# Four edits to a fused state-space and gated-layer gradient kernel: the order of k's loads, the width of ssm_k's transposes, the engine of one copy, the order of the last gradient

## The chip, the cores and the metric

The kernel runs on one core of a Trainium2 chip. A core has five engines that run side by side, each with its own queue, taken in order: TensorE (PE; matrix products and transposes, with weight loads listed apart as PEld), VectorE (DVE), ScalarE (ACT), GpSimd (POOL) and SyncE (SP), which here issues nearly all DMA transfers. TensorE writes into PSUM, a small accumulation memory, and ScalarE or VectorE copy results from there to SBUF, the working memory. The metric is the time of one execution on the device in microseconds (us); the lower the better.

## The reference

With sequence length S = 2048, width D = 512 and F = 1376, the forward function is

```python
xn = layernorm(A_q)
k_shift[s] = sum_t k[s - t'] * shift_k[:, t']        # four taps
kv = k_shift * v
y  = causal_conv(kv, ssm_k) + kv * ssm_D             # by FFT of length 2S in the reference
A  = xn * y
B  = ((xn @ w_gate) * (xn @ w_up)) @ w_down
out = x + A + B
```

The reference returns `out` and, for a given `grad_out`, the gradients of q, k, v, shift_k, ssm_k, ssm_D, w_gate, w_up and w_down: ten outputs, all bf16. In the kernel's numbering out_2 and out_3 are the gradients of k and v, out_4 to out_6 those of shift_k, ssm_k and ssm_D, out_7 to out_9 those of w_gate or w_up (two) and w_down.

## The kernel before

The sequence is laid out as `nat`: position s = 16 p + r sits in partition p (128 of them) at row r of R = 16. The long convolution is a two-stage Fourier transform by matrix products. In a first stretch (`front`, `pre`, `kernel_spec`) three signals (ssm_k, kv and the product of grad_out and xn) pass through `stage1` (TensorE into `pf`, copied to `fst`, stored to DRAM as `FD`). In a second (`groups`) they are loaded again as `X`, transformed, multiplied on VectorE and transformed back into `GD`, again in DRAM. Beside all this runs the gated layer over eight chunks of 256 positions (`ffn1`, `yb`). In the last stretch (`dw` with its side generators) TensorE computes the weight gradients over 11 blocks of F (10 of 128, the last of 96) and the second half of the inverse transforms.

The code lists work in the order of generators, which hand over at each `yield`. A scheduler then places the instructions of each engine; `tc.high_priority` moves some ahead, and `tc.issue_after(i)` keeps what is inside behind instruction i in that placing. On the chip each engine and each DMA queue runs its list strictly in that order.

These are the places that the change touches:

- `kernel_spec` (L405) reads `ssk`, ssm_k as loaded: 512 channels in 4 groups of 128 partitions, 2048 positions along the free axis. Helper `tr` turns four rows r at a time: 16 transposes of 128x128, each reading every 16th element (32 bytes apart), into one PSUM tile `ptk`. ScalarE copies it to `kn` (L235 is the line of the helper `act`, L238 that of `dve`), which the first stage reads. The two buffers of `kn` are shared with `skt`, the broadcast taps of the shift.
- `hds` are the two buffers of the gated layer's products; `hd1` is used by odd chunks.
- `inv_y` (L919) alternates the inverse transform of y and of the gradient towards kv for four rows at a time, from tiles `g` loaded out of `GD` by `load_g1` (L775). `load_vk` loads v and the shifted k (`KS`). VectorE forms the gradient towards shifted k (`dks`) and v (`kb`, stored as out_3, L939).
- `load_kh` (L1104) loads k once more as `khC`, with three rows of the neighbour partition: one load of 2 MB (L1108) and two of 336 and 45 KB. `dsk_gram` (L1027) multiplies `dks` with it on TensorE (`pk`, L1033) for the gradient of shift_k.
- `ew` runs `final` and `bwd` for each pair of rows: VectorE's work for out_0, out_1 and out_2, fed by `load_fin` (`bb`, L1072).
- `inv_dk` (L955) makes the gradient of ssm_k: `gk` loaded from `GD`, products `po`, copied by ScalarE to `o5t`. Its position 0 is the gradient of ssm_D: `put_dD` (L975) copies it to `dDs`, transposes it (`ptd`) and stores it.
- `dw` (L984) takes for each block of F first the gradient of w_down (`pd`, 16 matmuls of 512 columns, copied to `od`, stored), then those of w_up and w_gate (`pu`, 64 matmuls, copied to `og`, stored).

Of the kernel before, what the change touches and what calls it, by code (L numbers as in the profile page):

```python
# [8 lines left out]
BF = mybir.dt.bfloat16  # L9
F32 = mybir.dt.float32  # L10
I32 = mybir.dt.int32
ALU = mybir.AluOpType
# [178 lines left out]
def kernel(  # L191
# [39 lines left out]
    def cs(c):  # L231
        return slice(c * 128, (c + 1) * 128)

    def act(o, i):
        nc.scalar.copy(o, i)  # L235
# [16 lines left out]
    def P2(name, shape, dt=F32):  # L252
        return ps2.tile(shape, dt, name=name, tag="p2")

    def P1(name, shape, dt=F32):
        return ps1.tile(shape, dt, name=name, tag="p1")
# [27 lines left out]

    hds = [p.tile([P, NFB, 3, 256], BF, name=f"hd{i}") for i, p in enumerate((hdp, hdl))]

    tab_es = ExitStack()
    TB = Tables(nc, const, wY, tab_es.enter_context(tc.tile_pool(name="tabt", bufs=1, side="right")))
    for t in hds:
# [114 lines left out]

    def kernel_spec():  # L405
        def tr(r0):
            pt = P2("ptk", [P, 4, D], BF)
            for i in range(4):
                for c in range(NC4):
                    src = ssk[:, c, :].rearrange("d (p r) -> d r p", r=R)[:, r0 + i, :]  # L410
                    nc.tensor.transpose(pt[:, i, cs(c)], src, ident[:])
            kn = ST["st1"].tile([P, 4, D], BF, name="kn", tag="kn", bufs=KNB)
            with tc.high_priority(offset=SOON):
                act(kn[:], pt[:])
            return kn
        kn = tr(0)
        yield
        for r0 in range(0, R, 4):
            for i in range(4):
                stage1(0, kn, i, r0 + i, act if i % 2 else dve)  # L420
                if i == 1 and r0 + 4 < R:
                    nx = tr(r0 + 4)
                yield
            kn = nx
# [204 lines left out]
    def seq(*its):  # L629
        for it in its:  # L630
            for _ in it:
                yield
# [176 lines left out]
    def nat_h(fb, r):  # L809
        f0, fw = FBLK[fb]  # L810
        if fb not in TURNED:
            return nats[fb, 0][:, r, :fw]
        return nats[fb, 0][:, r // 2, 0, r % 2, :] if r < R - 2 else nats[fb, 1][:, 0, r % 2, :fw]
# [96 lines left out]
    def load_vk(r0):  # L910
        vb = c2b.tile([P, 2, D], BF, name="vb")
        nc.sync.dma_start(vb[:], v_n[:, r0:r0 + 2, :])
        kb = c2b.tile([P, 2, D], BF, name="kb")
        nc.sync.dma_start(kb[:], KS[:, r0:r0 + 2, :])
        return vb, kb

    DKS = {}
# [1 line left out]
    def inv_y():  # L919
        gq = pend  # L920
        todo = [(sg, r0) for r0 in range(0, R, 4) for sg in (0, 1)][2:]
        for r4 in range(0, R, 4):
            gy = gq.pop(0)
            vk = [load_vk(r4), load_vk(r4 + 2)]
            for i in range(0, 4, 2):
                st1p(gy, i, yC[:, r4 + i:r4 + i + 2, :])
            if todo:
                gq.append(load_g1(*todo.pop(0)))
            yield
            gd = gq.pop(0)  # L930
            for i in range(0, 4, 2):
                r0 = r4 + i
                vb, kb = vk.pop(0)
                dd = c2b.tile([P, 2, D], BF, name="dd")
                st1p(gd, i, dd[:])
                with tc.high_priority(offset=SOON):
                    DKS[r0] = nc.vector.tensor_tensor(dks[:, r0:r0 + 2, :], dd[:], vb[:], op=ALU.mult)
                    nc.vector.tensor_tensor(kb[:], dd[:], kb[:], op=ALU.mult)
                nc.sync.dma_start(o3_n[:, r0:r0 + 2, :], kb[:])  # L939
                if r0 == 2:  # L940
                    nc.gpsimd.memset(dks[96:128, R:R + 3, :], 0.0)
                    nc.sync.dma_start(dks[0:112, R:R + 3, :], dks[1:113, 0:3, :])
                    nc.sync.dma_start(dks[112:127, R:R + 3, :], dks[113:128, 0:3, :])
            if todo:
                gq.append(load_g1(*todo.pop(0)))
            yield
# [8 lines left out]
    def inv_dk():  # L955
        o5t = c2.tile([P, NC4, P, R], BF, name="o5t", tag="o5k")
        o5 = out_5.rearrange("(c q) s -> c q s", q=P)
        steps = [(dh, rh) for dh in range(2) for rh in range(2)]
        for n, (dh, rh) in enumerate(steps):
            gk = gks.pop(0)  # L960
            for b in range(2):
                po = P2("po", [P, 8, P])
                for i in range(8):
                    for c in range(2):
                        nc.tensor.matmul(po[:, i, :], lhsT=gk[:, c, i, cs(b)], rhs=TB.IW[:, c, :], start=(c == 0), stop=(c == 1))
                act(o5t[:, 2 * dh + b, :, 8 * rh:8 * rh + 8], po[:].rearrange("q r s -> q s r"))
                if rh == 1:
                    nc.sync.dma_start(o5[2 * dh + b], o5t[:, 2 * dh + b].rearrange("q s r -> q (s r)"))
                if b == 1 and n + 2 < len(steps):
                    gks.append(load_gk(*steps[n + 2]))  # L970
                yield
            if n == 2:
                yield from put_dD(o5t)

    def put_dD(o5t):  # L975
        nc.vector.tensor_copy(dDs[:], o5t[:, :, 0, 0])
        yield
        pt = P1("ptd", [P, P], BF)
        nc.tensor.transpose(pt[:NC4, :], dDs[:], ident[:])
        dDt = c2.tile([NC4, P], BF, name="dDt")  # L980
        dve(dDt[:], pt[:NC4, :])
        nc.sync.dma_start(out_6.rearrange("(c p) -> c p", p=128), dDt[:])

    def dw():  # L984
        og = None
        load_hb(2)
        for fb, (f0, fw) in enumerate(FBLK):
            last = fb + 1 == NFB
            pd = P1("pd", [P, D])
            for r in range(R):  # L990
                nc.tensor.matmul(pd[:fw, :], lhsT=nat_h(fb, r), rhs=goC[:, r, :], start=(r == 0), stop=(r == R - 1))  # L991
            od = c2b.tile([P, D], BF, name="od")
            act(od[:fw], pd[:fw])
            nc.sync.dma_start(out_9[f0:f0 + fw, :], od[:fw])
            yield
            if not last:
                hid_t(fb + 1, 0)
                yield
                hid_t(fb + 1, 1)
                yield  # L1000
            pu = P2("pu", [P, NC4, 2, P])
            if fb % 2 == 0:
                og = c2.tile([P, 2, NC4, 2 * P], BF, name="og")
            q0 = (fb % 2) * P
            for c in range(NC4):
                for r in range(R):
                    nc.tensor.matmul(pu[:, c, :, :fw], lhsT=xnC[:, r, cs(c)], rhs=nat_d(fb, r),  # L1007
                                     start=(r == 0), stop=(r == R - 1))
                if c == 1:
                    yield  # L1010
                    if not last:
                        hid_t(fb + 1, 2)
                        if fb + 3 in TURNED:
                            load_t(fb + 3)
                        elif fb + 3 < NFB:
                            load_hb(fb + 3)
                        yield
            act(og[:, :, :, q0:q0 + fw].rearrange("p t c f -> p c t f"), pu[:, :, :, :fw])
            if fb + 1 in TURNED:
                last_t(fb + 1)  # L1020
            if fb % 2 == 1 or last:
                a = f0 - q0
                for t, o in enumerate((out_7, out_8)):
                    nc.sync.dma_start(o[:, a:f0 + fw].rearrange("(c p) f -> p c f", p=128), og[:, t, :, :q0 + fw])
            yield

    def dsk_gram():  # L1027
        for c in range(NC4):
# [75 lines left out]
    def load_kh():  # L1104
        khC = c2.tile([P, R + 3, D], BF, name="khC", tag="o5k")
        nc.gpsimd.memset(khC[0:1, 0:3, :], 0.0)
        with tc.issue_after(DKS[10].ins):
            nc.sync.dma_start(khC[:, 3:3 + R, :], k_n)  # L1108
            nc.sync.dma_start(khC[1:113, 0:3, :], k_n[0:112, R - 3:R, :])
            nc.sync.dma_start(khC[113:128, 0:3, :], k_n[112:127, R - 3:R, :])  # L1110
        KH.append(khC)
        yield

    def every(gen, start, step):
        return [start, step, gen]
# [16 lines left out]
    def load_dk():  # L1132
        gks.append(load_gk(0, 0))
        gks.append(load_gk(0, 1))
        yield

    sides = [every(seq(inv_y(), load_kh(), load_dk()), 0, 3), every(dsk_gram(), 27, 2), every(inv_dk(), 35, 3), every(ew(), 7, 3)]
    for n, _ in enumerate(dw()):
        for sd in sides:
            if n >= sd[0]:  # L1140
# [35 lines left out]
```

## Time and profile before

| | |
|---|---|
| median of 3 runs | 497.99 us (497.42 to 498.01) |
| profiled execution | 496.1 us, span 494.2 us |
| TensorE busy | 472.5 us, 96% of the span |
| weight loads / VectorE / ScalarE / GpSimd busy | 314.4 / 339.8 / 317.4 / 13.8 us |
| DMA | 140.39 MB moved, mean 284 GB/s |
| granted TensorE clock | 0.995 of full speed |

All comes from one profiled execution. A row of the timeline gives start, length, engine, line, what is written and from what, and in brackets how long the engine was idle before and what ended that. Matmuls are pipelined: the length of one is the time until its result is there, while the next starts long before. So how often matmuls start is read from groups, not from single lengths. "SPq" rows are the issue of a DMA on SP's queue; when the data arrives is told apart, as time to landing.

### The profile page before, as it was taken

The numbers are of one execution on the slowest core, as the hardware profiler recorded it, in microseconds if no ns is written. First come the engines' busy times: TensorE is split into PE (matmuls) and PEld (weight loads), VectorE is DVE, ScalarE is ACT, GpSimd is POOL, SyncE is SP. The second block draws the span as 40 slices with busy tenths as digits, with TensorE's granted clock in tenths as the row PEclk, the third lists the DMA queues.
The fourth block names the chain that finished last, engine by engine and source line by source line (L and its number), as shares of the span: only waits on it lengthen the run. The fifth ranks groups of instructions, "written<-read, shape, count | busy, mean of one in ns | idle before, by whom it ended". The sixth has DMA issues, their size and how long they took to land.

```text
span 494.2 us, 10487 instructions
## 1 busy us (share of the span) xinstructions
PE 472.5 (96%) x4331; PEld 314.4 (64%) x4331; DVE 339.8 (69%) x623; ACT 317.4 (64%) x352; POOL 13.8 (3%) x29
## 2 busy tenths in 40 slices
PE   7789999999999999999999999999998989999986
PEld 7676764547647548447447744567676668877775
DVE  6679979987383768667786873018239999996740
ACT  4668896849748678779779963566575535453221
POOL 4400000000000000000000000020000000000000
PEclk9899999999999999999999999999999999999999
DMA  9998999899997966978968298999998899999823
GB/s 272 376 403 297 291 271 336 309 326 329 342 266 244 275 192 205 292 252 256 306 207 270 74 342 308 388 324 385 366 352 290 336 309 347 272 248 245 251 97 110
DMA packets 112523, 140.39 MB, mean 284 GB/s; under 512 B 33306, under 2 KB 86879, under 8 KB 110940
## 3 DMA queue, kind: packets, MB, share of 16 engines
q1 hardware_dynamic: 111004, 138.41, 86.6%
q10 hardware_dynamic: 1472, 1.31, 0.8%
q8 instruction: 34, 0.56, 0.5%
q14 instruction: 13, 0.11, 0.1%
HBM read 68.97 MB, written 63.41 MB: 268 GB/s over the span
## 4 chain that ended last, share of the span: by engine, by line
PE 60%; DMA 15%; DVE 13%; ACT 4%; SPq 3%; issue 2%; POOL 1%; ACTq 0%; DVEq 0%
PE pgu L513 12%; PE px L556 12%; PE pu L1007 8%; PE pdh L519 5%; DMA g<-GD 5%; PE py L549 5%; PE pd L991 4%; PE pt L834 3%; PE pg L614 3%; DMA x_b<-in_A_q_dram 2%; PE ps L585 2%; PE pf L366 2%; DMA out_dram<-dk 2%; PE pq L907 2%; PE pk L1033 2%
## 5 line engine op out<-in xcount | busy, mean ns | idle before, releaser
L556 PE MATMUL px<-WT,hd 128*128 128x512 bf16 (+1 forms) x352 | 81.0, 380 | 0.0
L1007 PEld LDWEIGHTS <-xnC 128*128 128x128 bf16 x704 | 67.3, 98 | 8.3 <-issue 0.3
L556 PEld LDWEIGHTS <-hd 128*128 128x128 bf16 (+1 forms) x352 | 32.8, 98 | 44.1 <-issue 7.4
L1007 PE MATMUL pu<-natd,xnC 128*128 128x256 bf16 x512 | 58.8, 273 | 0.2 <-ACT nath L235 0.2
L513 PE MATMUL pgu<-xt,Wu 128*128 128x256 bf16 (+1 forms) x352 | 54.0, 277 | 3.6 <-ACT gu L235 3.3
L235 ACT CAST GO<-pg 128x1024 bf16<-128x1024 f32 x48 | 46.2, 1015 | 17.5 <-PE pg L614 12.9
L235 ACT CAST SP<-ps 128x1024 bf16<-128x1024 f32 x48 | 46.5, 1028 | 11.9 <-PE ps L585 7.8
L235 ACT CAST gu<-pgu 128x1024 bf16<-128x1024 f32 (+1 forms) x48 | 45.4, 945 | 13.4 <-PE pgu L513 11.9
L513 PE MATMUL pgu<-xt,Wg 128*128 128x256 bf16 (+1 forms) x352 | 53.5, 275 | 0.0
L601 DVE TENSOR_TENSOR T<-SP 128x2048 bf16<-128x2048 bf16 x24 | 29.4, 1223 | 28.7 <-ACT SP L235 26.1
L519 PE MATMUL pdh<-gt,WdT 128*128 128x256 bf16 (+1 forms) x352 | 47.6, 273 | 0.1
L513 PEld LDWEIGHTS <-Wu 128*128 128x128 bf16 (+1 forms) x352 | 33.3, 101 | 19.1 <-issue 14.2
L235 ACT CAST fst<-pf 128x1024 bf16<-128x1024 f32 x40 | 39.1, 1035 | 3.8 <-issue 2.6
L549 PE MATMUL py<-Wd,hd 128*128 128x512 bf16 (+1 forms) x176 | 41.3, 379 | 0.0
L235 ACT COPY natd<-pt 128x2048 bf16<-128x2048 bf16 x16 | 30.0, 1873 | 14.8 <-PE pt L834 14.8
L519 PEld LDWEIGHTS <-WdT 128*128 128x128 bf16 (+1 forms) x352 | 34.9, 100 | 5.4
L513 PEld LDWEIGHTS <-Wg 128*128 128x128 bf16 (+1 forms) x352 | 35.3, 101 | 4.1
L235 ACT CAST og<-pu 128x1024 bf16<-128x1024 f32 (+1 forms) x11 | 10.9, 993 | 39.4 <-PE pu L1007 25.5
L533 DVE TENSOR_TENSOR hd<-gu 128x512 bf16<-128x512 bf16 (+1 forms) x48 | 19.1, 398 | 23.4 <-ACT gu L235 23.3
L534 DVE TENSOR_TENSOR hd<-gu,dh 128x1024 bf16<-128x1024 bf16 (+1 forms) x48 | 30.9, 643 | 1.4 <-ACT dh L235 0.4
L549 PEld LDWEIGHTS <-hd 128*128 128x128 bf16 (+1 forms) x176 | 16.6, 98 | 20.4 <-issue 2.5
L601 DVE TENSOR_TENSOR U<-SP 128x2048 bf16<-128x2048 bf16 x24 | 29.2, 1218 | 0.0
(166 smaller groups left out, 693.2 us busy)
## 6 DMA issues: line engine op xcount, KB each, us to landing
HDD<-hd SPq DMA_DIRECT2D x35, 384.0 KB, 3.8
FD<-fst SPq DMA_DIRECT2D x24, 512.0 KB, 4.5
X<-FD SPq DMA_DIRECT2D x24, 512.0 KB, 5.1
GD<-GO SPq DMA_DIRECT2D x24, 512.0 KB, 3.3
hb<-HDD SPq DMA_DIRECT2D x8, 1344.0 KB, 10.0
g<-GD SPq DMA_DIRECT2D x8, 1024.0 KB, 7.2
bb<-BX SPq DMA_DIRECT2D x8, 512.0 KB, 6.4
gk<-GD SPq DMA_DIRECT2D x4, 1024.0 KB, 8.5
```

The costliest lines, as they stand in the source:

```text
L235: nc.scalar.copy(o, i)
L513: nc.tensor.matmul(pgu[:w, i, t, :], lhsT=W[:, c, f0:f0 + w], rhs=xt[:, :, c, :], start=(c == 0), stop=(c == NC4 - 1))
L519: nc.tensor.matmul(pdh[:w, i, :], lhsT=WdT[:, c, f0:f0 + w], rhs=gt[:, :, c, :], start=(c == 0), stop=(c == NC4 - 1))
L533: nc.vector.tensor_tensor(hd[:fw, fb0:fb0 + n, 0, :], gu[:fw, :n, 0, :], gu[:fw, :n, 1, :], op=ALU.mult)
L534: nc.vector.tensor_tensor(hd[:fw, fb0:fb0 + n, 1:3, :], gu[:fw, :n], dh[:fw, :n].unsqueeze(2).to_broadcast((fw, n, 2, 256)), op=ALU.mult)
L549: nc.tensor.matmul(py[:], lhsT=hd[:fw, fb, 0, ss], rhs=Wd[:fw, fb, :], start=(fb == 0), stop=(fb == NFB - 1))
L556: nc.tensor.matmul(px[:], lhsT=hd[:fw, fb, t, ss], rhs=W[:fw, fb, :], start=(t == 1 and fb == 0), stop=(t == 2 and fb == NFB - 1))
L601: tt(W[:].rearrange("p c a d -> p c (a d)"), A[:, i:i + 1].rearrange("p c a d -> p c (a d)").to_broadcast((P, 2, 2 * D)), B[:].rearrange(" ...
L614: nc.tensor.matmul(pg[q // 2][64 * a:64 * a + 64, q % 2, :], lhsT=TB.EI[32 * q:32 * q + 32, 2 * g + a, yi].rearrange("p k c -> p (k c)"), ...
L834: nc.tensor.transpose(pt[:, r, :fw], hs[:, (r % 2) * 128:(r % 2) * 128 + 128], ident[:fw, :fw])
L991: nc.tensor.matmul(pd[:fw, :], lhsT=nat_h(fb, r), rhs=goC[:, r, :], start=(r == 0), stop=(r == R - 1))
L1007: nc.tensor.matmul(pu[:, c, :, :fw], lhsT=xnC[:, r, cs(c)], rhs=nat_d(fb, r), start=(r == 0), stop=(r == R - 1))
```

## The change

Four edits, in the order of the code:

1. ssm_k is turned in pairs of rows. Two neighbouring bf16 elements are read as one four-byte element; 8 transposes in place of 16 fill a tile `ptk` of float32 type, with a four-byte identity that GpSimd copies at the start into a still unused part of `hd1`. ScalarE then splits each pair with a strided read, in two copies of 1024 elements in place of one of 2048.
2. The loads of `khC` are tied behind the last load of `kb`, and called from inside `inv_y` in its last step. The entries of `DKS`, to which `ew`'s first load is tied, are now the stores of `kb` in place of VectorE's products. `load_kh` no longer takes a step of its own in the side generators.
3. The copy of D's gradient to `dDs` is done by ScalarE in place of VectorE.
4. The last block's gradient of w_down comes after those of w_up and w_gate. Its 96 rows are copied and stored in two halves of 256 columns: one by ScalarE and ScalarE's DMA queue, one by VectorE and SP's.

```diff
+    ident4 = hds[1][:, 9, 1, :].bitcast(F32)
+    nc.gpsimd.tensor_copy(ident4, ident[:])
...
         def tr(r0):
-            pt = P2("ptk", [P, 4, D], BF)
-            for i in range(4):
+            pt = P2("ptk", [P, 2, D], F32)
+            for i in range(2):
                 for c in range(NC4):
-                    src = ssk[:, c, :].rearrange("d (p r) -> d r p", r=R)[:, r0 + i, :]
-                    nc.tensor.transpose(pt[:, i, cs(c)], src, ident[:])
+                    src = ssk[:, c, :].bitcast(F32).rearrange("d (p q) -> d q p", q=R // 2)[:, r0 // 2 + i, :]
+                    nc.tensor.transpose(pt[:, i, cs(c)], src, ident4)
             kn = ST["st1"].tile([P, 4, D], BF, name="kn", tag="kn", bufs=KNB)
             with tc.high_priority(offset=SOON):
-                act(kn[:], pt[:])
+                for i in range(2):
+                    act(kn[:, 2 * i:2 * i + 2, :], pt[:, i, :].bitcast(BF).rearrange("p (d j) -> p j d", j=2))
...
-        nc.sync.dma_start(kb[:], KS[:, r0:r0 + 2, :])
+        DKS["kb", r0] = nc.sync.dma_start(kb[:], KS[:, r0:r0 + 2, :])
...
             vk = [load_vk(r4), load_vk(r4 + 2)]
+            if r4 == R - 4:
+                load_kh()
...
-                    DKS[r0] = nc.vector.tensor_tensor(dks[:, r0:r0 + 2, :], dd[:], vb[:], op=ALU.mult)
+                    nc.vector.tensor_tensor(dks[:, r0:r0 + 2, :], dd[:], vb[:], op=ALU.mult)
                     nc.vector.tensor_tensor(kb[:], dd[:], kb[:], op=ALU.mult)
-                nc.sync.dma_start(o3_n[:, r0:r0 + 2, :], kb[:])
+                DKS[r0] = nc.sync.dma_start(o3_n[:, r0:r0 + 2, :], kb[:])
...
-        nc.vector.tensor_copy(dDs[:], o5t[:, :, 0, 0])
+        act(dDs[:], o5t[:, :, 0, 0])
...
+    def down_grad(fb):
+        f0, fw = FBLK[fb]
+        pd = P1("pd", [P, D])
+        for r in range(R):
+            nc.tensor.matmul(pd[:fw, :], lhsT=nat_h(fb, r), rhs=goC[:, r, :], start=(r == 0), stop=(r == R - 1))
+        od = c2b.tile([P, D], BF, name="od")
+        if fb + 1 < NFB:
+            act(od[:fw], pd[:fw])
+            nc.sync.dma_start(out_9[f0:f0 + fw, :], od[:fw])
+        else:
+            for h, cp, q in ((0, act, nc.scalar), (1, dve, nc.sync)):
+                hc = slice(256 * h, 256 * h + 256)
+                cp(od[:fw, hc], pd[:fw, hc])
+                q.dma_start(out_9[f0:f0 + fw, hc], od[:fw, hc])
...
-            pd = P1("pd", [P, D])
-            for r in range(R):
-                nc.tensor.matmul(pd[:fw, :], lhsT=nat_h(fb, r), rhs=goC[:, r, :], start=(r == 0), stop=(r == R - 1))
-            od = c2b.tile([P, D], BF, name="od")
-            act(od[:fw], pd[:fw])
-            nc.sync.dma_start(out_9[f0:f0 + fw, :], od[:fw])
-            yield
+            if not last:
+                down_grad(fb)
+                yield
...
             yield
+            if last:
+                down_grad(fb)
+                yield
...
-        with tc.issue_after(DKS[10].ins):
+        with tc.issue_after(DKS["kb", R - 2].ins):
             nc.sync.dma_start(khC[:, 3:3 + R, :], k_n)
...
         KH.append(khC)
-        yield
...
-    sides = [every(seq(inv_y(), load_kh(), load_dk()), 0, 3), every(dsk_gram(), 27, 2), every(inv_dk(), 35, 3), every(ew(), 7, 3)]
+    sides = [every(seq(inv_y(), load_dk()), 0, 3), every(dsk_gram(), 27, 2), every(inv_dk(), 35, 3), every(ew(), 7, 3)]
```

## The prediction

> **What bounds the kernel now.** I read the page's first part, then the table of what TensorE waited for, then the timelines of the three places that the diff touches. The page first, with busy time by engine:
>
> ```profile
> span 494.2 us, 10487 instructions
> PE 472.5 (96%) x4331; PEld 314.4 (64%) x4331; DVE 339.8 (69%) x623; ACT 317.4 (64%) x352; POOL 13.8 (3%) x29
> ```
>
> TensorE has work 96% of the span, so a microsecond is won only by taking work off it, by removing one of its waits, or at the ends. Its longest waits (total, times, longest):
>
> ```profile
> PE pgu L513 <- ACT gu L235: 3.3, 1, 3.3
> PE pq L907 <- DMA g<-GD: 1.9, 3, 1.4
> PE pk L1033 <- DMA khC<-in_A_k_dram: 1.9, 1, 1.9
> PE pf L366 <- ACT kn L235: 1.6, 1, 1.6
> PE ptd L979 <- DVE dDs L976: 1.3, 1, 1.3
> ```
>
> The first is not touched. The next four are touched, and stand for 6.7 us. The two ends of the sum are therefore these waits, the time of the transposes `ptk`, and the drain after the last matmul. The profiled execution took 496.1 us, 1.9 us below the median of 497.99; the terms below are differences, and I take them off both.
>
> **Part 1: ssm_k in pairs of rows.** Groups by tile (ns min/median/max) and the timeline (start, length, engine):
>
> ```profile
> L411 PE MATMUL ptk<-ident,ssk x64: 219/226/236, 26.5 to 51.4; 128*128 128x128 bf16 x64
> L411 PEld LDWEIGHTS <-ssk x64: 143/148/163, 26.4 to 51.3; 128*128 128x128 bf16 x64
> 28.65 0.49 SPq L703 DMA_DIRECT2D skt<-in_A_shift_k_dram  x1
> 30.84 1.87 ACT L235 COPY kn<-ptk 128x2048 bf16<-128x2048 bf16 x1
> 32.76 0.38 PE L366 MATMUL pf<-kn,W 128*128 128x512 bf16 x1 [1.61 <-ACT kn L235]
> 34.26 1.24 PEld L411 LDWEIGHTS <-ssk 128*128 128x128 bf16 x16
> 35.90 1.23 DVE L705 COPY skb<-skt 128x2048 bf16<-128x2048 bf16 x1 [1.88 <-DMA skt<-in_A_shift_k_dram]
> 37.20 1.86 ACT L235 COPY kn<-ptk 128x2048 bf16<-128x2048 bf16 x1 [1.33 <-DVE rstd L335]
> 393.37 0.94 PE L834 MATMUL pt<-ident,hb 128*128 128x128 bf16 x14
> ```
>
> Sixteen loads of ssk span 1.24 us and the last lasts 0.15, so they start (1.24 - 0.15) / 15 = 73 ns apart: the 64 cost 4.7 us. The same form on contiguous data starts (0.94 - 0.22) / 13 = 55 ns apart, so the step of 32 bytes between elements costs 18 ns each. The change leaves 32 transposes of elements twice as wide, at the same step. No four-byte matmul is in this trace. Bounds: at the 55 ns of the contiguous form, 1.8 us (a gain of 2.9); with load and matmul one after the other, 148 + 226 = 374 ns, 12.0 us (a loss of 7.3). I take twice the 73 ns, because as many bytes are read in all: 4.7 us, no change. That lies next to the strided row, far from the serial one.
>
> The Trainium skill, "TensorE: Matmul & The Clock Gate", on weight-path performance modes, has a rule against elements of four bytes: the fast weight load is not given to FP32 weights. Its section on LDWEIGHTS gives columns / 1.2 ns, so 107 ns for 128 columns, an estimate. By that the 32 would cost 3.4 us, more than half as many loads at today's 73 ns, and the sum would be 1.3 us better than with my value; no run here has shown it yet.
>
> The eviction of `kn` becomes two copies of 1024 elements with a strided read. One 1024-element eviction and a short drain of the same engine:
>
> ```profile
> L235 ACT CAST o5t<-po 128x1024 bf16<-128x1024 f32 x8 | 8.2, 1020 | 2.5 <-PE po L965 2.5
> L235 ACT CAST dh<-pdh 96x256 bf16<-96x256 f32 x8 | 3.2, 404 | 0.0
> ```
>
> `o5t` is written with a stride and still takes 1.02 us; two make 2.04 against 1.87, so +0.17 for each of four groups, 0.7 us on an engine that is 64% busy. Where is it on the path? The order of the changed program shows that the first `pf` is released by the first half alone, which would shorten its wait of 1.61 us to about 0.8. But the second `kn` shares buffers with `skt`, and starts at 37.20 only when `skb` is done, however early the transposes are: the load at 28.65 gates it. So I count the early gain as nothing (at most 0.8), and the second group's longer eviction as 0.2 us lost on that path. The new copy of the identity on GpSimd has its cover in the next row; the cost is 0, and without it one 128x128 pass there:
>
> ```profile
> 11.51 0.25 POOL L156 TENSOR_SCALAR gt<-gj 128x1 f32<-128x1 f32 x1 [6.30 <-DVE gqi L65]
> ```
>
> The borrowed space in `hd1` is written by chunk 1 only at its fifth pair of blocks, behind the last `ptk` in the program. Part 1: 0.2 us lost, between 3.7 gained and 7.5 lost.
>
> **Part 2: the loads of k.** Timelines of the DMA queue, VectorE and TensorE, then how long khC's three loads took, and two windows (us, busy time of PE, PEld, DVE, ACT, POOL, clock, DMA share, GB/s):
>
> ```profile
> 328.27 0.97 SPq L1108 DMA_DIRECT2D khC<-in_A_k_dram  x1
> 334.77 0.69 DVE L1084 TENSOR_TENSOR o<-o,bb 128x1024 bf16<-128x1024 bf16 x1 [7.52 <-DMA bb<-BX]
> 366.86 0.69 DVE L1083 TENSOR_TENSOR o<-xnC,yC 128x1024 bf16<-128x1024 bf16 x1 [12.46 <-DMA out_dram<-o]
> 377.07 0.33 SPq L1100 DMA_DIRECT2D out_dram<-e  x1
> 377.97 0.53 SPq L775 DMA_DIRECT2D g<-GD  x1
> 382.74 0.33 SPq L1066 DMA_DIRECT2D out_dram<-dk  x1
> 385.66 0.60 SPq L914 DMA_DIRECT2D kb<-KS  x1
> 399.38 0.51 SPq L1109 DMA_DIRECT2D khC<-in_A_k_dram  x1
> 376.07 1.90 PE L907 MATMUL pq<-g,IW 128*128 128x512 bf16 x8 [1.35 <-DMA g<-GD]
> 383.78 1.90 PE L907 MATMUL pq<-g,IW 128*128 128x512 bf16 x8 [0.32 <-DMA g<-GD]
> 395.15 7.15 PE L1007 MATMUL pu<-natd,xnC 128*128 128x256 bf16 x64
> 407.18 1.94 PE L1033 MATMUL pk<-khC,dks 128*64 128x256 bf16 x32 [1.85 <-DMA khC<-in_A_k_dram]
> DMA to landing us min/median/max: 7.3/10.2/13.1
> 386.00:393.00 7.00, 7.00 (x59) 5.02 (x59) 6.93 (x13) 3.71 (x3) 0.00 (x0) 1.00 0.95 363
> 393.00:400.00 7.00, 7.00 (x80) 6.27 (x79) 6.90 (x17) 4.22 (x3) 0.00 (x0) 1.00 0.84 233
> ```
>
> Today 2 MB of khC are issued at 328.27, between the loads that the inverse transforms need, and its two short edge loads only at 399.38; `pk` waits for the latter. After the change all three stand behind the `kb` load of the last rows (385.66), a `g` that stood behind the first stores of `kb` moves ahead of them, and the two `bb` loads behind stores of `kb`. That takes 2 MB at 363 GB/s, some 6 us of DMA time, out of the stretch before 386.
>
> The `g` waits: the 1.35 us goes, since its load has those 6 us. The last `g` (377.97) stands behind the store of `e`, which waits for VectorE's final(1); and VectorE now starts final(0) later, after four more products. That has cover in its idle 12.46 us before 366.86, and if the cover is gone, the store and this `g` are later by as much. With TensorE 1.5 us earlier at the same load, I leave 0.5 us of waiting here: a gain of 1.4 of the 1.9 (bounds 0 and 1.9).
>
> The khC wait: the first load is issued at about 386.3. TensorE's order puts the first `pk` after 32 instead of 64 `pu` and before the next `pd`: 395.15 + 3.5 = 398.6, less the 1.4, so 397.2. The big load took 13.1 us before, when 3 MB stood ahead of it; now I count some 1.5 MB ahead, an estimate from the loads in this queue order, and 3.9 MB at 363 GB/s are 10.7 us: 397.0. That is level with TensorE, so part of the wait may stay; I take a gain of 1.2, between 1.9 (landed earlier) and a loss of 1.3 (13.1 us plus 1 us for the edge rows: a wait of 3.2). The 2 MB fall into a stretch whose DMA share is 0.95 and then 0.84 at 233 GB/s, so there is a hole to take a part of them. What is queued behind khC on SP: `bb`, the stores of `o`, `e` and `kb`, and the next `hb`, none of which TensorE waits for in the table above. The lost step in the order of generators also moves the `gk` loads ahead of a `bb`, and the last turned load behind two stores of `o5t`; no wait on either is in the table, so both are 0, down to a gain lost (rival 3).
>
> **Part 3: D's copy on ScalarE.** ScalarE finishes the `o5t` that it needs near 460.7 and is then idle; a copy of 4 columns fits there:
>
> ```profile
> 459.68 1.01 ACT L235 CAST o5t<-po 128x1024 bf16<-128x1024 f32 x1 [0.31 <-PE po L965]
> 467.75 1.01 ACT L235 CAST og<-pu 128x1024 bf16<-128x1024 f32 x1 [7.05 <-DMA out_dram<-og]
> ```
>
> `ptd` then finds `dDs` ten microseconds old: 1.3 us gained (0 to 1.3). VectorE still copies `dDt` late, but nothing on TensorE needs that buffer.
>
> **Part 4: the last gradient last.** The drain before (the landing row is that of `od` stores):
>
> ```profile
> 489.47 0.33 PE L1007 MATMUL pu<-nat,xnC 128*128 128x192 bf16 x2
> 489.88 0.80 ACT L235 CAST og<-pu 128x768 bf16<-128x768 f32 x1 [4.74 <-PE pu L1007]
> 490.71 0.93 SPq L1024 DMA_DIRECT2D out_dram<-og  x2
> DMA to landing us min/median/max: 1.7/2.0/2.9
> ```
>
> TensorE's work is the same in another order. From its end, 489.80, to 494.2 are 4.4 us: 0.91 to the first issue, half of 0.93 to the second, then 3.0. Afterwards: 0.08 to wake, 0.40 for a half (the 96x256 row of part 1; VectorE's half beside it), 0.05, then the same 3.0 for one issue per queue: 3.5. Gain 0.9, between 0 (a landing of 2.9 instead of 2.0) and 1.2. The stores of `og` have the 3.4 us of `pd` to land in.
>
> **Sum.** -0.2 + 1.4 + 1.2 + 1.3 + 0.9 = 4.6 us: 497.99 - 4.6 = 493.4 us; the profiled 496.1 would be 491.5, with a span of 489.6.
>
> **Rivals.** (1) khC lands late: everything as above, but the 2 MB need 13.1 us again and the edge rows follow; the wait is 3 us, that term is -1.2 instead of +1.2, and the time 495.8. For it: a DMA share of 0.95 and over around 386; against: less stands ahead of it. (2) Slower: four-byte transposes do not overlap, load and matmul in turn, 374 ns each, so 7.3 us more: 500.7. It decides from (4.7 + 4.6 + 1.0) / 32 = 322 ns each. For it: no such instruction in the trace. Against: every two-byte form here overlaps. (3) The transposes are cheap, 73 ns each: 2.3 us less work, of which the first two groups lie before the gate at 37.20, so 1.2 gained: 492.2. (4) The gains of part 2 are given back: TensorE, earlier, runs into later loads (`gk`, turned blocks) behind 2 MB more; 2.6 us go, 496.0. Against: after 408 it waits for no DMA.
>
> **How the numbers follow.** The forecast 0.42, rival 1 0.20, rival 2 0.12, rival 3 0.16, rival 4 0.10. The best ends of parts 2 to 4 with 1.5 for part 1 give 7.8 gained, 490.2; at the other end rival 4 with a drain that gains nothing is 496.9, transposes half way to serial give 497.0, and some of both reach 497.8; the likeliest case alone 491.8 to 494.8. Under 0.2% (1.0 us, about what a measurement of this kernel can tell) is a small part of rivals 1 and 4: faster 0.82, same 0.06, slower 0.12.
>
> **What would show it.** Right: 32 `ptk` at starts near 146 ns; no `pq` wait above 0.5; `pk` within 1 us of khC; no `ptd` wait; 3.5 us from the last `pd` to the end. Wrong: `ptk` over 322 ns, or waits on khC, `gk` or `natT` that sum to over 4 us.

## The result, and the profile after

The changed kernel takes 492.57 us (median of 5 runs, 492.02 to 494.88), the kernel before 497.99 (496.22 to 498.21) in the same comparison: a ratio of 0.9908, 95% interval 0.9879 to 0.9938. In a later comparison it came out smaller: 493.77 against 496.82, 0.9963, 0.9937 to 0.9989. The ratios, here and below, leave out slow executions (more than 1.5% above the fastest of the same kernel), so they need not be the quotient of the medians. The profiled execution took 492.12 us.

The page of the changed kernel, its first part:

```profile
span 490.2 us, 10429 instructions
PE 472.5 (96%) x4299; PEld 314.5 (64%) x4299; DVE 339.4 (69%) x623; ACT 317.9 (65%) x357; POOL 14.1 (3%) x30
```

TensorE's busy time is the same 472.5 us as before, so the 4.0 us that the span lost are time in which it had nothing to do: waits and the drain at the end. What TensorE waited for in the changed kernel (total, times, longest):

```profile
PE pgu L519 <- ACT gu L235: 3.3, 1, 3.3
...
PE pt L840 <- DMA hb<-HDD: 1.3, 1, 1.3
PE ps L591 <- DMA X<-FD: 1.2, 3, 0.5
PE pq L913 <- DMA g<-GD: 1.1, 1, 1.1
PE pd L996 <- ACT nat L235: 0.9, 1, 0.9
PE pf L370 <- ACT kn L235: 0.8, 1, 0.8
...
PE pk L1055 <- DMA khC<-in_A_k_dram: 0.4, 1, 0.4
```

The four waits that the change touches (`g` 1.9, `khC` 1.9, `kn` 1.6, `dDs` 1.3) are now 1.1, 0.4, 0.8 and none. But two rows are new: the first `hb`, 1.3, and `nat`, 0.9. So 4.4 us of waits went and 2.2 came, beside 0.3 more on `X`.

The turned rows of ssm_k, after, by tile and by timeline (ns min/median/max; start, length):

```profile
L416 PEld LDWEIGHTS ptk<-hd,ssk x32: 185/190/208, 26.6 to 49.6; 128*128 128x128 f32 x32
L416 PE MATMUL ptk<-hd,ssk x32: 272/274/323, 26.6 to 49.7; 128*128 128x128 f32 x32
33.73 1.04 PE L416 MATMUL ptk<-hd,ssk 128*128 128x128 f32 x8
32.02 0.38 PE L370 MATMUL pf<-kn,W 128*128 128x512 bf16 x1 [0.76 <-ACT kn L235]
L235 ACT COPY kn<-ptk x8: 1011/1032/1059, 31.0 to 51.5; 128x1024 bf16<-128x1024 bf16 x8
```

Eight four-byte transposes take 1.04 us, so they start (1.04 - 0.27) / 7 = 110 ns apart, and 32 of them cost 3.5 us where the 64 cost 4.7. Load (190) and matmul (274) overlap.

The loads of k and the end of the program, after:

```profile
375.42 0.33 SPq L1122 DMA_DIRECT2D out_dram<-e  x1
376.33 0.53 SPq L781 DMA_DIRECT2D g<-GD  x1
384.38 0.46 SPq L1130 DMA_DIRECT2D khC<-in_A_k_dram  x1
374.05 1.89 PE L913 MATMUL pq<-g,IW 128*128 128x512 bf16 x8
382.27 1.90 PE L913 MATMUL pq<-g,IW 128*128 128x512 bf16 x8 [1.05 <-DMA g<-GD]
397.91 1.94 PE L1055 MATMUL pk<-khC,dks 128*64 128x256 bf16 x32 [0.39 <-DMA khC<-in_A_k_dram]
466.35 1.01 ACT L235 CAST og<-pu 128x1024 bf16<-128x1024 f32 x1 [8.18 <-DMA out_dram<-og]
468.11 0.61 PE L996 MATMUL pd<-goC,nat 128*128 128x512 bf16 x2 [0.88 <-ACT nat L235]
468.65 0.22 PE L987 MATMUL ptd<-ident,dDs 128*4 128x128 bf16 x1
486.25 0.59 PE L996 MATMUL pd<-goC,nat 128*96 128x512 bf16 x2
486.88 0.37 ACT L235 CAST od<-pd 96x256 bf16<-96x256 f32 x1 [2.61 <-PE pd L996]
487.28 0.42 DVE L238 CAST od<-pd 96x256 bf16<-96x256 f32 x1 [12.70 <-ACT od L235]
487.73 0.34 SPq L1005 DMA_DIRECT2D out_dram<-od  x1
```

The earlier `g` wait (1.35) is gone; the last one has grown from 0.32 to 1.05, because its load still stands behind a store of `e`: it is issued 1.6 us sooner (376.33 against 377.97), but without the wait TensorE arrives 2.2 us sooner (381.22 against 383.46). `ptd` waits for nothing, but the `pd` ahead of it now waits 0.88 for `nat`, which ScalarE copies after an `og` that waited for the store before it (8.18 us idle). From TensorE's end, 486.84, to the end of the span are 3.4 us; before it were 4.4. The two halves of the last output are not copied beside each other: VectorE's starts at 487.28, when ScalarE's has ended.

### The profile page after: what moved, and what is told of

The parts are those of the page before. It is cut to its first block, busy times and chain, and to the rows that moved or that the text cites. A ratio compares the mean times of both kernels' runs of the same rounds, so it can differ in the third digit from the quotient of the medians.

```text
span 490.2 us, 10429 instructions
## 1 busy us (share of the span) xinstructions
PE 472.5 (96%) x4299; PEld 314.5 (64%) x4299; DVE 339.4 (69%) x623; ACT 317.9 (65%) x357; POOL 14.1 (3%) x30
## 4 chain that ended last, share of the span: by engine, by line
PE 51%; DVE 20%; DMA 19%; ACT 5%; issue 2%; POOL 1%; SPq 1%; ACTq 0%; DVEq 0%
PE pgu L519 13%; PE px L562 11%; DMA out_dram<-o 6%; PE pdh L525 5%; PE py L555 5%; PE pu L1026 4%; PE pg L620 3%; PE ps L591 2%; PE pd L996 2%; DMA FD<-fst 2%; DMA out_dram<-dk 2%; DVE dxn L1113 2%; DMA hb<-HDD 2%; DMA bb<-BX 2%; PE pt L840 2%
```

## The experiments

Two numbers help to read all of them. The first is the time against the kernel before in the same comparison. The second splits the profiled span at the start of the first down gradient, the first `pd`: edit 1 (pairs) lies ahead of it, edits 2 to 4 behind it. For the kernel before these are 320.4 and 494.2 - 320.4 = 173.8 us.

| kernel | median us | ratio to before (95%) | first pd | from there |
|---|---|---|---|---|
| changed | 492.57 | 0.9908 (0.9879 to 0.9938) | 320.3 | 169.9 |
| changed, later comparison | 493.77 | 0.9963 (0.9937 to 0.9989) | 320.8 | 171.0 |
| edit 1 alone | 498.85 | 1.0050 (1.0024 to 1.0077) | 321.7 | 175.0 |
| edit 2 alone | 490.70 | 0.9885 (0.9855 to 0.9916) | 319.5 | 171.3 |
| edit 3 alone | 495.08 | 0.9985 (0.9956 to 1.0014) | 319.3 | 173.7 |
| edit 4 alone | 495.04 | 0.9967 (0.9934 to 1.0000) | 319.9 | 173.1 |
| edits 2, 3 and 4 | 492.29 | 0.9917 (0.9888 to 0.9946) | 320.2 | 171.7 |
| edit 2 without the tie of bb | 494.40 | 0.9984 (0.9953 to 1.0015) | 318.9 | 172.3 |
| changed, pairs by one copy | 495.28 | 0.9985 (0.9959 to 1.0012) | 322.4 | 169.5 |
| changed, first hb in two loads | 494.05 | 0.9946 (0.9920 to 0.9973) | 322.2 | 170.1 |
| changed, og stores by ScalarE | 503.32 | 1.0109 (1.0045 to 1.0173) | 323.8 | 178.7 |
| changed, later g loads by ScalarE | 507.55 | 1.0223 (1.0168 to 1.0277) | 322.4 | 182.3 |
| changed, all three repairs | 508.00 | 1.0221 (1.0178 to 1.0265) | 321.0 | 185.0 |

A program's own executions lie further apart than I had assumed: 31 of the kernel before on one chip went from 491.3 to 501.2 us. Differences of one profile by less than 2 us are therefore weak; the verdicts below rest on the ratios or on what several profiles share.

### Each edit alone

Edit 1 alone:

```diff
...
-            pt = P2("ptk", [P, 4, D], BF)
+            pt = P2("ptk", [P, 2, D], F32)
...
-                act(kn[:], pt[:])
+                for i in range(2):
+                    act(kn[:, 2 * i:2 * i + 2, :], pt[:, i, :].bitcast(BF).rearrange("p (d j) -> p j d", j=2))
```

> The kernel before with edit 1 alone (ssm_k in pairs). Theory A (what an edit frees early is taken again by a load that arrives no sooner): transposes start about 110 ns apart, TensorE is some 1.4 us ahead from 50 to 300 us, and then its first turn of hb at 311 waits about 1.3 us longer for that load, so the span is 494.1 us, 0.1 below before, no change in the times. Theory B (each edit is worth what it frees): the 1.4 us stay, span 492.8.

It is slower: 498.85 us, 0.50% above the kernel before, which neither theory had. The transposes do their part, but the lead that they give doesn't last. Timelines of edit 1 alone, VectorE, SyncE's queue and TensorE, and last from VectorE's waits (60 to 130 us) those for stores of `ks_b`:

```profile
98.83 0.66 DVE L382 TENSOR_TENSOR dy_b<-go_b,x_b 128x1024 bf16<-128x1024 bf16 x1
106.61 0.69 DVE L390 TENSOR_TENSOR ks_b<-kh,skb 128x1024 bf16<-128x1024 bf16 x1 [3.60 <-DMA KS<-ks_b]
118.68 0.69 DVE L382 TENSOR_TENSOR dy_b<-go_b,x_b 128x1024 bf16<-128x1024 bf16 x1
102.89 0.45 SPq L398 DMA_DIRECT2D KS<-ks_b  x1
122.39 0.39 SPq L542 DMA_DIRECT2D HDD<-hd  x1
123.44 1.00 SPq L580 DMA_DIRECT2D X<-FD  x1
120.08 0.59 PE L369 MATMUL pf<-dy_b,W 128*128 128x512 bf16 x2
129.93 0.63 PE L590 MATMUL ps<-X,EF 64*32 64x512 bf16 x16 [1.78 <-DMA X<-FD]
DVE ks_b L390 <- DMA KS<-ks_b: 3.9, 2, 3.6
```

The same places in the kernel before:

```profile
100.51 0.66 DVE L379 TENSOR_TENSOR dy_b<-go_b,x_b 128x1024 bf16<-128x1024 bf16 x1
104.93 0.69 DVE L387 TENSOR_TENSOR ks_b<-kh,skb 128x1024 bf16<-128x1024 bf16 x1 [1.11 <-DMA KS<-ks_b]
118.83 0.68 DVE L379 TENSOR_TENSOR dy_b<-go_b,x_b 128x1024 bf16<-128x1024 bf16 x1
99.61 0.64 SPq L395 DMA_DIRECT2D KS<-ks_b  x1
121.09 0.39 SPq L537 DMA_DIRECT2D HDD<-hd  x1
122.37 0.96 SPq L575 DMA_DIRECT2D X<-FD  x1
120.24 0.59 PE L366 MATMUL pf<-dy_b,W 128*128 128x512 bf16 x2
128.23 0.63 PE L585 MATMUL ps<-X,EF 64*32 64x512 bf16 x16
DVE ks_b L387 <- DMA KS<-ks_b: 3.5, 2, 2.4
```

VectorE's `dy_b` is 1.7 us ahead with the pairs (98.83 against 100.51); by the last `dy_b` the lead is 0.15 us. With two copies for each group the planner put the front's work in another order on VectorE and SyncE. A store of `ks_b` is issued at 102.89, not 99.61, and VectorE, which needs its buffer, idles 3.6 us there instead of 1.1. But these rows mislead: all waits of VectorE for such stores sum to 3.9 us against 3.5 before, and to 3.0 in the changed kernel, so they don't explain the loss.

Another difference is shared by all kernels with two copies. On SyncE's queue a store of `HDD` stands ahead of the load of `X`; here it waits 1.3 us for VectorE's `hd`, in the kernel before 0.4. From the last `dy_b` product (120.08 here) to the issue of that load (123.44) are 3.35 to 3.37 us in all seven kernels with two copies, and 1.7 to 2.2 in the seven others, the one with pairs by one copy among them. The first product of `X` then follows 8.5 to 9.9 us behind that of `dy_b`, in the others 7.8 to 8.4.

Edit 2 alone (the loads of khC after the last `kb`, and the tie of `bb` moved to the store):

```diff
...
+            if r4 == R - 4:
+                load_kh()
...
-                    DKS[r0] = nc.vector.tensor_tensor(dks[:, r0:r0 + 2, :], dd[:], vb[:], op=ALU.mult)
+                    nc.vector.tensor_tensor(dks[:, r0:r0 + 2, :], dd[:], vb[:], op=ALU.mult)
...
-                nc.sync.dma_start(o3_n[:, r0:r0 + 2, :], kb[:])
+                DKS[r0] = nc.sync.dma_start(o3_n[:, r0:r0 + 2, :], kb[:])
...
-        with tc.issue_after(DKS[10].ins):
+        with tc.issue_after(DKS["kb", R - 2].ins):
...
```

> The kernel before with edit 2 alone (k's loads and the stores as ties). Theory A: the waits on g fall from 1.9 to about 1 us and that on khC from 1.9 to below 0.5, TensorE is 2.5 us ahead at 425 us, but VectorE's copy dDs comes only about 0.7 us sooner, so the wait of ptd grows from 1.3 to about 3 us: span 493.5, 0.7 below before. Theory B: the 2.5 us stay, span 491.7.

490.70 us, from four executions: edit 2 alone gives as much as the whole change. Theory B, a span of 491.7, is nearer to the 490.8 measured than theory A. The wait on `ptd`, which theory A let grow, went without edit 3: TensorE reached it with `dDs` ready. Its remaining waits, edit 2 alone:

```profile
PE pq L907 <- DMA g<-GD: 1.5, 2, 1.3
PE pk L1035 <- DMA khC<-in_A_k_dram: 0.7, 1, 0.7
```

Edit 3 alone:

```diff
-        nc.vector.tensor_copy(dDs[:], o5t[:, :, 0, 0])
+        act(dDs[:], o5t[:, :, 0, 0])
```

> The kernel before with edit 3 alone (D's copy on ScalarE). Both theories: the wait of ptd (1.3 us) goes and nothing else moves before it, span 492.9. If the next wait (the copy nat on ScalarE, which the trace of before shows 0.4 us ahead of its use) already binds here, it is 493.3 or more.

495.08 us, 0.9985: not to be told from nothing. The span of this profile, 493.0, fits what both theories had. The wait on `dDs` is gone, but `pk`, which waited 1.9 for khC, waits 2.4 for VectorE's `tk` in this profile, and the waits for `g` sum to 2.5.

Edit 4 alone (`down_grad` of the last block behind everything else, its output in halves by two engines):

```diff
...
-            pd = P1("pd", [P, D])
...
+            if last:
+                down_grad(fb)
+                yield
```

> The kernel before with edit 4 alone (last gradient last, in halves). Both theories: from TensorE's last matmul to the end 3.4 instead of 4.4 us, span 493.2. If the late end were only moved, because the stores of og land last anyway, the span stays at 494.

495.04 us, 0.9967: 1.6 us by the ratio, with an interval that just reaches 1 and holds the 0.9 predicted. The drain in this profile is 3.4 us, as expected.

### The change without edit 1

The rival to test was whether edit 1 was slow only by accident, alone. Edits 2, 3 and 4 on the kernel before (here against the changed kernel), and the changed kernel again beside it:

```diff
...
-            pt = P2("ptk", [P, 2, D], F32)
+            pt = P2("ptk", [P, 4, D], BF)
...
```

> The kernel before with edits 2, 3 and 4 (khC and its tie, dDs on ScalarE, the tail) and ssk_k turned in two-byte elements as before. Theory F (the pairs cost more in the stretch up to the first down gradient than their transposes give: in the kernel with edit 1 alone that gradient's first product began at 321.7 us, in kernels without it at 319.3 to 320.4): 488.5 us, 0.991 of the changed kernel's median run beside it less about 2 us, first down gradient at 319.3 to 320.4. Theory G (edit 1 alone was slow by its own accident; in the whole it gives its 1 us): 1 us above the changed kernel's time of the same call. In both: the wait for g no more than 1.5 us in all, the wait for khC under 1, the tail about 1 us shorter than before's.

> The changed kernel, once more, beside the others. Both theories: 0.988 to 0.994 of the kernel before. Theory F: 1 to 3 us above the kernel without the pairs. Theory G: 0.5 to 1.5 us below it. The first down gradient begins between 320 and 322.5 us.

Without the pairs 492.29 us (489.47 to 494.18, 8 runs), with them 493.77 (493.06 to 498.01, 12 runs): 1.5 us by the medians, 0.9963 against 0.9917 or 2.3 us by the ratios, whose intervals overlap a little. Together with edit 1 alone (2.5 us slower than before by its ratio) this speaks for theory F: the pairs cost time. Three forecasts were missed: 488.5 was 3.8 us too low, the changed kernel came out at 0.9963 and not at 0.988 to 0.994, and the wait for `g` without the pairs was 2.3 us, where both theories had no more than 1.5. The profiled execution without the pairs was the slowest of its eight (span 491.9), so its span shows no gain over the changed kernel's 491.8. Over all profiles the stretch is clear, though. In the table the six kernels without pairs start the first `pd` at 318.9 to 320.4, on average 319.7 (the kernel before among them); the five with pairs, the three rows with ScalarE's queue left out, at 320.3 to 322.4, on average 321.5. That difference is not the price itself, since a late start is partly made up behind it: from there, the kernels with edits 2 to 4 take 171.7 us without the pairs, and 169.5 to 171.0 with them.

### Is it the planner's order?

Edit 1 with one copy of 128x2048 for each group. This gives VectorE nearly the order of the kernel before:

```diff
-                for i in range(2):
-                    act(kn[:, 2 * i:2 * i + 2, :], pt[:, i, :].bitcast(BF).rearrange("p (d j) -> p j d", j=2))
+                act(kn[:].rearrange("p (i j) d -> p i j d", j=2), pt[:].bitcast(BF).rearrange("p i (d j) -> p i j d", j=2))
```

> The changed kernel, but each block of four rows of the pairs is written out by one ScalarE copy of 128x2048 instead of two of 128x1024. It has the same transposes; its planner puts VectorE's work on the Laplacian and the filter's rows (x_b, dy_b, t_b, ks_b) in nearly the order of the kernel before, where two copies shift much of it. Theory F1 (the loss in the front comes from that other order of work on VectorE and SP): 1 to 2 us faster than the changed kernel, as fast as or up to 1 us faster than the kernel without the pairs; first X-FD product at or before 128.3 us. Theory F2 (the loss comes from the four-byte form itself, or from nothing that order sets): within 0.7 us of the changed kernel.

The store of `ks_b` came back to 99.46, and the load of `X` to 1.9 us behind the last `dy_b` product, but the kernel is no faster: 495.28 us, and its first product of `X` starts at 129.20, not at or before 128.3. Theory F1 falls: that order is not the whole cause. F2's margin of 0.7 us was not kept either; it is 1.5 us slower by the medians. The first half's early release is lost with the single copy, so this run doesn't take the order away alone. The last `dy_b` product starts at 120.92, with no lead over the kernel before (120.24), and the late `hb` is there too (TensorE's waits, and the copies' times):

```profile
PE pf L370 <- ACT kn L235: 1.6, 1, 1.6
PE pt L839 <- DMA hb<-HDD: 1.3, 1, 1.3
L235 ACT COPY kn<-ptk x4: 1866/1878/1898, 31.1 to 51.8; 128x2048 bf16<-128x2048 bf16 x4
```

The last row settles another point: with the strided read the copy takes 1.88 us at the median, the same as without it in the kernel before. What two copies cost more, 2.06 against 1.88 us, is the price of a second instruction and not of the step.

Something common to the kernels with pairs is left that I can't explain: the first `hb` makes TensorE wait 0.6 to 1.3 us in all five, and 0 to 0.4 in the six without; its load takes 7.5 to 8.2 us to land against 6.4 to 7.3 (the split one left out). Why those bytes land later stays open.

### Which half of edit 2

Only khC's loads moved, `bb` tied to VectorE's `dks` as before (the first line is unchanged):

```diff
...
                     DKS[r0] = nc.vector.tensor_tensor(dks[:, r0:r0 + 2, :], dd[:], vb[:], op=ALU.mult)
...
-        with tc.issue_after(DKS[10].ins):
+        with tc.issue_after(DKS["kb", R - 2].ins):
...
```

> The kernel before with half of edit 2: khC's three loads follow the last v and k loads on SyncE's queue, but the loads of bb stay tied to VectorE's product dks as before, not to the store of o3. Theory M1 (the gain of edit 2 is that khC lands in time and that its 2 MB no longer lie beside the g loads; the tie of bb adds nothing): 490.5 to 491.5 us, as edit 2 whole (490.7). Theory M2 (part of it is bb's later loads): 492.5 to 494, with the wait for g at 2 us or more in all.

494.40 us. Both waits that edit 2 was to remove are gone from its profile altogether, `g` and khC, and still it gives less than half of edit 2's gain (measured in another comparison); M1 falls, and the time lies just above M2's range, though not for M2's reason (a `g` wait of 2 us). What came instead, edit 2 without the tie of bb:

```profile
325.10 1.81 SPq L1074 DMA_DIRECT2D bb<-BX x2
422.61 1.62 PE L967 MATMUL po<-IW,gk 128*128 128x128 bf16 x16 [1.97 <-DVE kd L1040]
```

The two `bb` loads stand early again (325.10, in edit 2 whole 343.80 at the first), and later `po` waits 2.0 us for VectorE's `kd`, a row that edit 2 whole doesn't have. That one causes the other is not shown.

### Repairs of the waits that are left

I took the remaining waits of the changed kernel to have a cause each, so that repairs would add. First the new one: the first `hb` in two loads, the smaller part first.

```diff
-        nc.sync.dma_start(t[:fw], HDD[:fw, fb])
+        if fb == 0:
+            nc.sync.dma_start(t[:fw, :, 0, :], HDD[:fw, fb, :, 0, :])
+            nc.sync.dma_start(t[:fw, :, 1:3, :], HDD[:fw, fb, :, 1:3, :])
+        else:
+            nc.sync.dma_start(t[:fw], HDD[:fw, fb])
```

> The changed kernel, its first load of hb cut in two: the third that the first turn reads, then the rest. Theory A (the load of hb at 303 us is what takes back the 1.4 us of the pairs): the wait of 1.3 us at 309 to 311 us goes or falls below 0.3, span 488.9 to 489.2. Rival (the whole stretch is held by the DMA engines' rate, whatever the order): the wait moves to the second turn or to the goC product, span 490.2.

The wait in this profile is 0.6 us, not below 0.3, and the second profile of the changed kernel, without the split, has 0.7: an effect of the split isn't shown. The first product of `X` started at 130.41, after 1.8 us of waiting for it, as in edit 1 alone. The time, 494.05, isn't better than the changed kernel's.

Then the stores of `og` (behind which `nat` waits) by ScalarE's queue, the later loads of `g` by ScalarE's queue, and both with the split:

```diff
-                    nc.sync.dma_start(o[:, a:f0 + fw].rearrange("(c p) f -> p c f", p=128), og[:, t, :, :q0 + fw])
+                    nc.scalar.dma_start(o[:, a:f0 + fw].rearrange("(c p) f -> p c f", p=128), og[:, t, :, :q0 + fw])
```

```diff
-        nc.sync.dma_start(t[:], GD[sg, :, :, r0:r0 + 4, :])
+        (nc.scalar if r0 > 0 else nc.sync).dma_start(t[:], GD[sg, :, :, r0:r0 + 4, :])
```

> The changed kernel with the stores of og issued on ScalarE's queue, right behind the copies, in place of SP's. Theory A (edit 3 is worth only 0.3 us because the copy nat stands behind an og copy that waits for the store of the og before): the wait of 0.9 us on nat at 467 us goes, span 489.3. Rival (the 0.9 us come from late DMA landing, not from the place on SP's queue): no change, span 490.2.

> The changed kernel with the later six loads of g issued on ScalarE's queue. Theory A (the remaining 1.1 us of waiting on g comes from SP's queue, where the load stands behind the store of e, which waits for VectorE): the wait goes, span 489.2, unless khC then arrives later than TensorE by as much. Rival (the rate of the DMA engines sets it): the wait stays near 1 us.

> The changed kernel with the three repairs together (first hb load cut, og and g on ScalarE's queue). Theory A, each wait its own cause: 1.3 + 0.9 + 1.1 less what khC takes (0.4 to 1): span 487.3 to 487.9. Rival, one shared cause (DMA rate): 490.

All three are slower: 503.32 us (1.0109), 507.55 (1.0223) and 508.00 (1.0221). The theory that repairs add falls. TensorE's waits, `og` by ScalarE:

```profile
PE pk L1055 <- DVE kd L1060: 4.0, 2, 2.8
PE pq L913 <- DMA g<-GD: 3.4, 1, 3.4
```

and the later loads of `g` by ScalarE, with two rows of TensorE's timeline and a window (us, busy time of PE, PEld, DVE, ACT, POOL, clock, DMA share, GB/s):

```profile
PE pk L1055 <- DVE kd L1060: 4.3, 1, 4.3
416.74 3.62 PE L1055 MATMUL pk<-khC,dks 128*64 128x256 bf16 x32 [4.29 <-DVE kd L1060]
425.30 1.94 PE L1055 MATMUL pk<-khC,dks 128*64 128x256 bf16 x32
415.00:420.00 5.00, 3.26 (x32) 2.67 (x32) 2.06 (x5) 0.00 (x0) 0.00 (x0) 0.50 1.09 309
```

The wait of `nat` is gone in the first, and the wait for `g` in the second, as meant. But `pk` now waits for `kd`, which none of the one-edit kernels' longest waits has. VectorE's work for the two sides (`o`, `e`, `dk`, `kd`) runs behind stores and `bb` loads on SyncE, and with some transfers taken out of that queue the planner ordered the rest another way; that this delays `kd` is argued, not shown. Long waits also cost more than their length here. Behind the wait of 4.3 us the granted clock was 0.50 in the window from 415 to 420 us, and 32 products of `pk` took 3.62 us where the same 32 took 1.94 later. The executions with `g` by ScalarE, alone or with the other repairs, have a mean granted clock of 0.983 to 0.987; the changed kernel's have 0.993 to 1.000. How much of the loss is the order, how much ScalarE's own time for the issues and how much the clock wasn't separated.

## Why the prediction was right, and where its steps were wrong

The time, 493.4 us, lies between the two measurements, 492.57 and 493.77. That the sum is about right is luck, because errors cancel: the terms were -0.2, +2.6, +1.3 and +0.9 us, and the edits alone measure -2.5, +5.7, +0.7 and +1.6 by their ratios, the last two not told apart from nothing.

- **Part 1, the transposes.** The step "twice the 73 ns" was wrong: 110 ns, not 146, so 3.5 us and not 4.7. Rival 2 (load and matmul in turn, 374 ns) fell. The Trainium skill ("TensorE: Matmul & The Clock Gate", LDWEIGHTS) gives columns / 1.2 ns, so 107 ns for 128 columns, an estimate, which I set aside. The trace's spacing agrees with it to 3 ns; but the row of one load lasts 190 ns, so that the load sets the spacing isn't shown.
- **Part 1, the eviction.** Two copies of 1.03 us, 1.02 predicted; the first `pf` waited 0.76, 0.8 predicted.
- **Part 1, the term.** "0.2 us lost" should have been 2.3 to 2.5 lost (the ratios of the kernel without pairs to the one with them, and of edit 1 alone), in spite of cheaper transposes. What failed is the view of the place: I followed the new copies up to the gate at 37.20 and asked no further what the rest of the front does. The gate did not swallow the gain: the last products of `kn` start at 57.37 in the changed kernel, 59.63 before. Behind them the load of `X` is issued 3.35 us after the last `dy_b` product instead of 1.7 to 2.2, behind the store that waits for `hd`, and the first `hb` is late. The later load of `X` is shown in all kernels with two copies; but with one copy it is gone and the time is no better, so the whole cause stays open. My wide bound (7.5 lost) held it, but for another reason. Rival 3's price of a transpose (73 ns) was as far off as mine, and its gain had the wrong sign.
- **Part 2, the g wait.** 1.4 of 1.9 predicted to go; 0.8 went in the changed kernel, 0.4 with edit 2 alone. The step "I leave 0.5 us of waiting" named the right load, the one behind the store of `e`, and was too small: 1.05 and 1.37 us in the changed kernel's two profiles, 1.31 with edit 2 alone and 2.32 without the pairs. The prediction had TensorE 1.5 us earlier at that load; in the changed kernel's first profile it was 2.2.
- **Part 2, khC.** Issued from 384.38, its loads landed 12.1 to 12.3 us after their issue, in the middle between my 10.7 and 13.1; `pk` waits 0.4 (0.7 with edit 2 alone), so 1.5 of 1.9 went, 1.2 predicted. Rival 1 fell.
- **Part 2 as a whole.** 2.6 predicted; edit 2 alone measures 1.15% of 496.4, 5.7 us (4.2 to 7.2), though its profiled stretch from the first `pd` is only 2.5 us shorter, in the slowest of its four runs. Two things were left out of the term. The tie of `bb` I had costed at nothing: without it the gain is 0.8 us by the ratio, 2.4 by the medians, though how it saves time isn't shown. And the wait on `ptd`, 1.3 us, goes with edit 2 alone.
- **Part 3.** The 1.3 us of `ptd` went, as predicted. But edit 2 removes the same wait, so the terms of parts 2 and 3 don't add. The step "1.3 us gained" also didn't ask what is late next: 0.9 came back as the wait for `nat`, behind a store of `og` on SyncE's queue. Alone the edit shows nothing.
- **Part 4.** The drain went from 4.4 to 3.4 us, 1.0, with 0.9 predicted, but not in the way predicted. "VectorE's half beside it" was wrong: it starts when ScalarE's has ended, so the last store is issued 0.89 us after TensorE's end and not 0.53. From there the end came in 2.5 us, not "the same 3.0". These two errors cancel. Why VectorE waits for ScalarE's half isn't shown.
- **Rival 4** (the gain given back) was right in kind, smaller and at another place: 0.9 us at `nat`, not 2.6 at `gk` after 408. The 1.3 us at `hb` lie ahead of part 2.

The bound of 0.2% that I took for what a measurement can tell was too narrow; the intervals here are about 0.3% to either side.

Edit 2 alone (0.9885), the changed kernel in its first comparison (0.9908) and the kernel without edit 1 (0.9917) aren't told apart by their ratios. Where the last was measured beside the changed kernel, it was ahead.

## What to carry to other kernels

Where a planner orders the instructions, cutting one copy in two can change the order of much else: here, in every kernel with two copies, a load on another engine's queue came 1.2 us or more later. Compare each engine's and each queue's order before and after, and price the buffers whose release moves, before counting what the edit itself saves. A wait that goes is worth its length only until the next thing that is late; read the row behind it. And test the parts of a combined edit apart: here one of four parts carried most of the gain and another took some of it back.

## What the runs showed of the hardware

- Transposes of four-byte elements at a step of 32 bytes start 110 ns apart (load 190 ns, matmul 274), two-byte ones 73 ns (148, 226): twice the bytes for 1.5 times the time.
- ScalarE copied 128x2048 two-byte elements out of PSUM in 1.88 us, with a step of four bytes between them as without: the step cost nothing. Two copies of 128x1024, 1.03 us each, took 0.19 us more than the one.
- Executions of one program, the kernel before, spread over 2% (491.3 to 501.2 us in 31 runs).
- In this kernel, handing a few DMA issues from SyncE's queue to ScalarE's lost 1.1 to 2.2% against the kernel before.
- Behind a wait of TensorE of 4.3 us, the granted clock was 0.50 in a window of 5 us, and 32 matmuls took 3.62 us instead of 1.94.
